# The copies of feed-forward pieces move behind the copy of M on ScalarE, their squares behind c1 on VectorE

## The chip, the cores and the metric

The kernel runs on one core of a Trainium2 chip. The metric is the device time of one execution in microseconds (us), as the median of a few runs. TensorE (PE) multiplies into PSUM; VectorE (DVE) and ScalarE (ACT) read PSUM and SBUF; GpSimd (POOL) works on SBUF only; SyncE (SP) issues DMAs. Each engine carries out its own instructions in the order in which the program issues them, and waits on semaphores for the others.

## What is computed

A recurrence over 768 time steps for 4 batches and 8 heads of size 40, and a feed-forward network behind it:

```
y[t]  = r[t] . state
Sa    = state . a[t]
state = state * w[t] - outer(Sa, b[t]) + outer(v[t], k[t])
x     = y, laid out as 3072 tokens x 320
out   = (relu(x @ w_in) ** 2) @ w_out        # 320 -> 2048 -> 320
```

The inputs and the output are float32. The kernel computes the recurrence in chunks of 128 time steps as matrix products with a triangular system per chunk, and holds most operands as bf16.

## The kernel before

**Tiling.** There are 6 chunks of time. In each chunk the 4 batches times 8 heads are worked off in 8 *steps* of 4 heads, so the main loop (line 490) runs over 48 steps, and two more that drain it. Tile's scheduler is switched off (`manual_schedule`): on every engine the instructions stand in the order in which the Python code issues them.

**A step** issues, in this order:

1. `st_ex_mm` and `st_a_mm`: products for the step before (`ex`, line 341) and for the next one (`ca`, line 242), on PE.
2. the first *filler*: one piece of feed-forward work.
3. `st_y`, `st_ex_ev` (DVE, lines 378, 383 and 349) and `st_z` (PE, line 358) for earlier steps.
4. `st_p`: the products P (PE, lines 258 and 264); `st_m`: ACT copies P to Mc (line 273). This is the "copy of M".
5. `prepare(st, 1)`: in even steps `prep_ga`, which transposes on PE (line 197), copies the result to GT on ACT (line 224) and makes AT from it on DVE (line 225), and `prep_cast` (ACT `lnW`, POOL casts); in odd steps `prep_rv`, which transposes and copies to RV on ACT (line 204, 1.02 us).
6. `st_corr` with Mc (PE, line 280); `st_c1`: DVE makes c1 from P and Mc (line 288); `st_a_ev`: DVE makes CN of the next step (line 250).
7. the second filler.
8. `st_corr` with c1 (PE, line 280); `st_sn`: ACT makes Sn, a part of EVX (line 296), POOL makes x and Cc (lines 299 and 300), ACT sums squares of CN into a junk tile jk (line 302); at the last step of a chunk two longer sums, jm (line 307), follow.
9. the third filler.
10. `prepare(st, 4)`: in even steps `prep_decay`, the product cs (PE, line 179), which ACT turns into GI and G (lines 182 and 184) and POOL into K and B (line 188); in odd steps `prep_kb`, transposes on PE and a copy to KBT on ACT (line 212).
11. `st_t`: transposes tb (PE, lines 316 and 322), the copy SnT (DVE, line 326), the copy UBD (ACT, line 328); `st_kb` (PE, line 368); the gather of X by DMAs on SP and the loads of later batches.

**Feed-forward work.** The output of a chunk goes through the network in two halves of 256 tokens. A half has 12 pieces, which the three fillers of four steps take one by one from step 8 on: eight pieces `ffn_in`, each six matmuls into a PSUM tile `hp` (line 428), a Relu copy by ACT to `hs` (line 433) and a square of `hs` into `Gt` (line 436; pieces 0, 2, 4, 6 on DVE, pieces 1, 3, 5, 7 on POOL); then two output tiles in two pieces each (`ffn_out`, line 454), with the copy `osb` by ACT (line 458) and an output DMA on SP after the second. Below, a step with the pieces 0 to 2 is of kind **A**, with 3 to 5 of kind **B**, with 6, 7 and the first half of an output tile of kind **C**, with the three other output pieces of kind **D**. Steps 8 to 47 are ten times A, B, C, D. The two halves of the last chunk are left: six pieces of the first run in steps 48 and 49, and all others after the loop, where six PSUM tiles are used in turn.

**Squares.** `ffn_in` puts its square in a list, and `flush` issues it when the next filler is called.

**PSUM.** All eight banks are taken. Two of them, the tag `ff`, serve the tiles `hp`, `op_`, `cs` and the transposes of `prep_rv`, `prep_kb` and `prep_ga` (t1, t2, t3). A new tile of that tag takes the bank whose last tile got its last reader first in program order, and its first matmul waits until that reader is done. In the kernel before the sequence is: A: hp, t3, hp, hp, cs; B: hp, t1, hp, hp, t2; C: hp, t3, hp, op_, cs; D: t1, op_, t2.

Of the kernel before, what the change touches and what calls it, by code (L numbers as in the profile page):

```python
# [8 lines left out]
BF16 = mybir.dt.bfloat16  # L9
I32 = mybir.dt.int32  # L10
ALU = mybir.AluOpType
ACTF = mybir.ActivationFunctionType
# [6 lines left out]
def kernel(  # L19
# [21 lines left out]
    nc = tc.nc  # L41

    NB, NHH, T, D = r.shape
    L = 128
# [11 lines left out]
    HB = NB // 2  # L56
# [5 lines left out]
    ffp = ctx.enter_context(tc.tile_pool(name="ffp", bufs=3))  # L62
# [23 lines left out]
    for m in range(AHEAD):  # L86
# [11 lines left out]
        out=UTI[:], in_=ones_f[:], pattern=[[1, 128]],  # L98
# [7 lines left out]
        out=IDb[:], in_=ones_b[:], pattern=[[1, 128]],  # L106
# [3 lines left out]
    for i in range(30):  # L110
# [4 lines left out]
        out=MEX[:], in_=MEX[:], pattern=[[0, 4], [1, L]],  # L115
# [15 lines left out]
    for i in range(4):  # L131
# [5 lines left out]
        for s in range(2):  # L137
            o_ = 64 * s
            nc.vector.tensor_copy(
                out=t_[o_:o_ + D, 0, :, L:LV],  # L140
                in_=IDb[o_:o_ + D, o_:o_ + D].rearrange("p (u d) -> p u d", u=1)
# [126 lines left out]
    def st_m(st):  # L268
        c, q = divmod(st, NQ)
        if q == 0:  # L270
            Mc[c] = chp.tile([128, NQ, 4, D], BF16, name="Mc", tag="Mc")
            Cc[c] = chp.tile([128, NQ, 4, D], BF16, name="Cc", tag="Cc")
        nc.scalar.activation(out=Mc[c][:, q], func=ACTF.Copy,
                             in_=Ps[st][:].rearrange("p i s e -> p (i s) e")[:, :, 0:D])
# [10 lines left out]
    def st_c1(st):  # L285
        c, q = divmod(st, NQ)
        c1 = c1s[st] = qdp.tile([128, 4, D], BF16, name="c1", tag="c1")
        nc.vector.tensor_tensor(out=c1[:],  # L288
                                in0=Ps[st][:].rearrange("p i s e -> p (i s) e")[:, :, 0:D],
                                in1=Mc[c][:, q], op=ALU.subtract)  # L290

    def st_sn(st):
        c, q = divmod(st, NQ)
        P, EVX, c1, CN = Ps.pop(st), EVXs[st % NEV], c1s.pop(st), CNs.pop(st)
        Sn = EVX[:, :, :, L + LV:2 * LV].rearrange("p i s e -> p (i s) e")
        nc.scalar.activation(out=Sn, in_=P[:].rearrange("p i s e -> p (i s) e")[:, :, 0:D],  # L296
                             func=ACTF.Copy, scale=-1.0)
        t_ = qdp.tile([128, 4, D], FP32, name="x1", tag="x1")
        nc.gpsimd.tensor_tensor(out=t_[:], in0=Mc[c][:, q], in1=c1[:], op=ALU.add)  # L299
        nc.gpsimd.tensor_tensor(out=Cc[c][:, q], in0=t_[:], in1=Sn, op=ALU.add)  # L300
        jk = qdp.tile([128, 2, 2, L], BF16, name="jk", tag="jk", bufs=1)
        nc.scalar.activation(out=jk[:], in_=CN[:, :, :, 1, :], func=ACTF.Square,  # L302
                             accum_out=ACC[:, AN + st:AN + st + 1])
        if q == NQ - 1:
            for src, at in ((Mc.pop(c), AM), (Cc.pop(c), AC)):
                jm = qdp.tile([128, NQ, 4, D], BF16, name="jm", tag="jm", bufs=1)
                nc.scalar.activation(out=jm[:], in_=src[:], func=ACTF.Square,  # L307
                                     accum_out=ACC[:, at + c:at + c + 1])
# [23 lines left out]
    def st_ex_mm(st):  # L332
        c, o, j0, p2, EVX = where(st)
        SnT = SnTs.pop(st)
        ex = exs[st] = [ps.tile([128, 2, 2, L], FP32, name=f"ex{s}", tag=f"ex{s}")
                        for s in range(2)]
        for u in range(2):
            for i in range(2):
                for s in range(2):
                    lhsT = SnT[half(s), i, :] if u else o.RV[half(s), 1, j0 + i, 0:L]  # L340
                    nc.tensor.matmul(out=ex[s][:, i, u, :], lhsT=lhsT,  # L341
                                     rhs=o.RV[half(s), 0, j0 + i, 0:L],
                                     start=(i == 0 and u == 0), stop=True, skip_group_check=True)

    def st_ex_ev(st):
        EVX = EVXs[st % NEV]
        ex = exs.pop(st)
        for s in range(2):
            nc.vector.tensor_tensor(  # L349
                out=EVX[:, :, s, 0:2 * LV].rearrange("p i (u x) -> p i u x", u=2)[:, :, :, 0:L],  # L350
                in0=ex[s][:], in1=MEX[:].rearrange("p (i u) x -> p i u x", u=2), op=ALU.mult)
# [59 lines left out]
            engines[h % len(engines)].dma_start(  # L411
                out=X[g][row:row + D], in_=src[:, HB * hf:HB * hf + HB, h // 2, :])

    later = []

    def flush():
        while later:
            later.pop(0)()

    def ffn_in(c, hf, jj):  # L420
        flush()
        if jj == 0:
            Gts[c, hf] = chp.tile([128, NJ, HB, L], BF16, name="Gt", tag="Gt")
        hp = ps.tile([128, 2, HB * L], FP32, name="hp", **where_ff())
        for u in range(2):
            j = 2 * jj + u
            for g in range(3):
                nc.tensor.matmul(out=hp[:, u, :], lhsT=WIN[g][0:rows[g], j * 128:(j + 1) * 128],  # L428
                                 rhs=Xs[c, hf][g][0:rows[g]].rearrange("p a b -> p (a b)"),
                                 start=(g == 0 and u == 0), stop=(g == 2),  # L430
                                 skip_group_check=True)
        hs = ffp.tile([128, 2 * HB * L], BF16, name="hs", tag="hs")
        nc.scalar.activation(out=hs[:], in_=hp[:].rearrange("p u x -> p (u x)"), func=ACTF.Relu)  # L433
        eng = nc.gpsimd if jj % 2 and not tail else nc.vector
        Gt = Gts[c, hf]
        later.append(lambda: eng.tensor_tensor(  # L436
            out=Gt[:, 2 * jj:2 * jj + 2].rearrange("p j a b -> p (j a b)"),
            in0=hs[:], in1=hs[:], op=ALU.mult))

    ops, tail = {}, []  # L440

    def where_ff():
        if not tail:
            return {"tag": "ff", "bufs": 2}
        tail.append(tail.pop(0))
        return {"tag": tail[-1], "bufs": 2} if tail[-1] == "ff" else {"tag": tail[-1]}

    def ffn_out(c, hf, b_, part):
        flush()
        if part == 0:  # L450
            ops[c, hf, b_] = ps.tile([128, DM], FP32, name="op_", **where_ff())
        op_ = ops[c, hf, b_]
        for j in range(part * NJ // 2, (part + 1) * NJ // 2):
            nc.tensor.matmul(out=op_[:], lhsT=Gts[c, hf][:, j, b_, :], rhs=WOUT[:, j, :],  # L454
                             start=(j == 0), stop=(j == NJ - 1))
        if part == 1:
            osb = ffp.tile([128, DM], FP32, name="osb", tag="osb")
            nc.scalar.activation(out=osb[:], in_=op_[:], func=ACTF.Copy)  # L458
            tok = (HB * hf + b_) * T + c * L
            nc.sync.dma_start(out=out[tok:tok + L, :], in_=osb[:])  # L460
# [5 lines left out]
    def filler(st):  # L466
        if fill and fill[0][0] <= st:
            fill.pop(0)[1]()
# [8 lines left out]
    def prepare(st, lot):  # L477
        for f, m in when.pop((st, lot), []):
            f(m)
# [10 lines left out]
    for st in range(NS + 2):  # L490
        if 1 <= st <= NS:
            st_ex_mm(st - 1)
        if st + 1 < NS:
            st_a_mm(st + 1)
        filler(st)
        if st >= 2:
            st_y(st - 2)
        if 1 <= st <= NS:
            st_ex_ev(st - 1)
            st_z(st - 1)  # L500
        if st < NS:
            st_p(st)
            st_m(st)
        prepare(st, 1)
        if st < NS:
            st_corr(st, Mc[st // NQ][:, st % NQ], False)
            st_c1(st)
        if st + 1 < NS:
            st_a_ev(st + 1)
        filler(st)  # L510
        if st < NS:
            st_corr(st, c1s[st], True)
            st_sn(st)
        filler(st)
        prepare(st, 4)
        st_t(st, st - 2)
        if 1 <= st <= NS:
            st_kb(st - 1)
        if st == 1:
            load_win()  # L520
        if st == 4:
            load_wout()
        if st >= 2:
            c, q = divmod(st - 2, NQ)
            hf = q // (NQ // 2)
            if q % (NQ // 2) == NQ // 2 - 1:
                gather(c, hf, [nc.sync] if st < NS + 1 else [nc.sync, nc.gpsimd, nc.sync])
                at = st + (3 if c + 1 < NCH else 2)
                fill += [(at, lambda c=c, hf=hf, j=j: ffn_in(c, hf, j)) for j in range(NJ // 2)]
                fill += [(at, lambda c=c, hf=hf, b_=b_, p_=p_: ffn_out(c, hf, b_, p_))  # L530
                         for b_ in range(HB) for p_ in range(2)]
        prepare(st, 5)
        if st == 3:
            nc.gpsimd.memset(UZs[0][:], 0.0)
    flush()


# [130 lines left out]
```

## Time and profile before

| | |
|---|---|
| time, median of 3 runs | 330.74 us (329.7 to 332.66) |
| the profiled execution | 330.49 us, span 328.8 us |
| busy PE / PE weight loads | 85% / 65% |
| busy DVE / ACT / POOL | 68% / 71% / 57% |
| granted PE clock, whole span | 0.943 |
| granted PE clock, 107 to 155, 155 to 203 and 203 to 251 us | 1.00 |
| eight steps (one chunk) in steady state | 48.0 us |
| PE busy in the 48.0 us from 155 to 203 us | 44.46 us |

The span is the profiled stretch from the first to the last instruction; the execution's own time is 1.7 us longer. Times in the timeline are microseconds from the start of the span. A line of the timeline gives start, length, engine, source line, operation, the tile written and the tiles read, the number of instructions merged, and in brackets how long the engine was idle before and what released it. Ends of matmuls are modelled, and a matmul may start before the one before it is said to end.

The two jm instructions of line 307 mark the end of a chunk: they begin at 155.0 and at 202.9 us, so steps 24 to 31 lie between. Of these, step 28 (kind A) has its first piece at 181.64 us, step 29 (B) at 187.26, step 30 (C) at 192.60, and step 31 (D) begins its first output piece at 198.65.

### The profile page before, as it was taken

What the parts mean: (1) busy time and instruction counts of PE and PEld (TensorE: products, weight loads), DVE (VectorE), ACT (ScalarE), POOL (GpSimd) and SP (SyncE); (2) the same over time, 40 slices, a digit from 0 to 9 for tenths busy, and PEclk for the clock granted to TensorE, in tenths of its full rate; (3) what the DMA queues carried; (4) which work ended last, traced back from release to release, by engine and by line L of the source; (5) the groups of instructions that cost most, each with busy time, mean ns of one, the idle gap of its engine ahead of it and who ended that gap; (6) DMA issues with size and microseconds to landing.
All of it is one profiled execution on the core that took longest, in us unless ns stands there. A gap on an engine that the chain in (4) does not pass through costs nothing.

```text
span 328.8 us, 10009 instructions
## 1 busy us (share of the span) xinstructions
PE 280.4 (85%) x3856; PEld 213.3 (65%) x3856; DVE 222.7 (68%) x545; ACT 232.8 (71%) x569; POOL 188.3 (57%) x342
## 2 busy tenths in 40 slices
PE   4478777799999799999799999899998899888990
PEld 3446555577777577777577777677776677666770
DVE  7226968587787587786686886686876775954430
ACT  3366766886886986887986787886887886538450
POOL 3367757296585485676476676476674673533300
PEclk9555978899999999999999999999999999999997
DMA  8992999985737437635736844735862701000100
GB/s 136 174 165 40 176 165 167 169 126 99 151 71 138 94 69 141 126 69 112 128 55 121 147 82 78 144 62 120 131 106 47 147 18 44 20 23 28 55 22 29
DMA packets 164187, 32.86 MB, mean 100 GB/s; under 512 B 158660, under 2 KB 163780, under 8 KB 164130
## 3 DMA queue, kind: packets, MB, share of 16 engines
q1 hardware_dynamic: 161586, 29.44, 49.7%
q0 software_dynamic: 2544, 2.68, 5.1%
q8 instruction: 32, 0.52, 0.7%
q14 instruction: 25, 0.20, 0.2%
HBM read 28.84 MB, written 3.93 MB: 100 GB/s over the span
## 4 chain that ended last, share of the span: by engine, by line
PE 56%; ACT 18%; issue 7%; DVE 7%; POOL 4%; DMA 3%; SPq 3%; ACTq 0%; DVEq 0%; POOLq 0%
PE hp L428 12%; PE t L197 6%; PE ex L341 4%; PE P L280 4%; PE cs L179 4%; ACT hs L433 3%; ACT jm L307 3%; PE uy L368 3%; ACT RV L204 3%; SPq L81 3%; PE tb L316 3%; PE ca L242 2%; DMA NV<-in_v_dram 2%; DVE c L288 2%; ACT GT L224 2%
## 5 line engine op out<-in xcount | busy, mean ns | idle before, releaser
L428 PE MATMUL hp<-X,WIN 120*128 120x256 bf16 (+1 forms) x576 | 78.9, 275 | 8.1 <-ACT osb L458 6.1
L433 ACT ACTIVATE hs<-hp 128x512 bf16<-128x512 f32 x96 | 57.3, 597 | 26.1 <-PE hp L428 22.7
L349 DVE TENSOR_TENSOR EVX<-ex,MEX 128x512 bf16<-128x512 f32 x96 | 61.8, 686 | 1.7 <-PE ex L341 0.5
L428 PEld LDWEIGHTS <-WIN 120*128 120x128 bf16 (+1 forms) x576 | 50.7, 98 | 18.9 <-issue 9.6
L250 DVE TENSOR_TENSOR CN<-ca,MCN 128x512 bf16<-128x512 f32 x96 | 61.4, 681 | 0.7 <-PE ca L242 0.7
L299 POOL TENSOR_TENSOR x<-Mc,c 128x160 f32<-128x160 bf16 x48 | 23.3, 486 | 66.7 <-DVE c L288 66.6
L436 POOL TENSOR_TENSOR Gt<-hs 128x512 bf16<-128x512 bf16 x43 | 48.4, 1125 | 9.9 <-ACT hs L433 9.6
L454 PEld LDWEIGHTS <-Gt 128*128 128x128 bf16 x384 | 34.3, 97 | 13.4 <-POOL Gt L436 0.8
L280 PEld LDWEIGHTS <-CN 128*128 128x128 bf16 x384 | 23.2, 98 | 27.2 <-issue 23.6
L326 DVE COPY SnT<-tb 128x256 bf16<-128x256 bf16 x48 | 14.0, 291 | 33.3 <-PE tb L322 27.6
L300 POOL TENSOR_TENSOR Cc<-x,EVX 128x160 bf16<-128x160 f32 x48 | 25.3, 527 | 17.1 <-ACT EVX L296 16.8
L436 DVE TENSOR_TENSOR Gt<-hs 128x512 bf16<-128x512 bf16 x53 | 27.4, 519 | 9.4 <-ACT hs L433 9.2
L225 DVE TENSOR_TENSOR AT<-t,GT 128x512 bf16<-128x512 bf16 x24 | 10.2, 425 | 31.4 <-ACT GT L224 31.4
L302 ACT ACTIVATE jk<-CN 128x512 bf16<-128x512 bf16 x48 | 30.1, 627 | 0.0
L212 ACT ACTIVATE KBT<-t 128x1024 bf16<-128x1024 bf16 x24 | 24.6, 1024 | 6.0 <-PE t L197 6.0
L204 ACT ACTIVATE RV<-t 128x1024 bf16<-128x1024 bf16 x24 | 24.6, 1023 | 5.1 <-PE t L197 3.0
L188 POOL TENSOR_TENSOR Kp<-NK,GI 128x320 bf16<-128x320 f32 x24 | 22.4, 933 | 6.6 <-ACT GI L182 5.6
L280 PE MATMUL P<-c,CN 128*128 128x40 bf16 x192 | 12.4, 181 | 13.5 <-DVE c L288 13.5
L288 DVE TENSOR_TENSOR c<-P,Mc 128x160 bf16<-128x160 f32 x48 | 15.3, 319 | 10.4 <-PE P L280 9.6
L378 DVE TENSOR_TENSOR YS<-uy,GT 128x256 bf16<-128x256 f32 x48 | 20.2, 421 | 1.2 <-PE uy L368 0.8
L242 PE MATMUL ca<-AT,KBT 64*128 64x128 bf16 x384 | 20.0, 228 | 1.2 <-DVE AT L225 1.2
L296 ACT ACTIVATE EVX<-P 128x160 bf16<-128x160 f32 x48 | 14.4, 300 | 8.7 <-PE P L280 8.4
(142 smaller groups left out, 636.6 us busy)
## 6 DMA issues: line engine op xcount, KB each, us to landing
NW<-in_w_dram SPq DMA_DIRECT2D x24, 160.0 KB
NK<-in_k_dram SPq DMA_DIRECT2D x24, 160.0 KB
NB<-in_b_dram SPq DMA_DIRECT2D x24, 160.0 KB
NA<-in_a_dram SPq DMA_DIRECT2D x24, 160.0 KB
NV<-in_v_dram SPq DMA_DIRECT2D x24, 160.0 KB
NR<-in_r_dram SPq DMA_DIRECT2D x24, 160.0 KB
out_dram<-osb SPq DMA_DIRECT2D x24, 160.0 KB
X<-YS SPq DMA_DIRECT2D x93, 20.0 KB
```

Of the source, the lines that this page charges most:

```text
L204: nc.scalar.activation(out=o.RV[:, :, :, 0:L], in_=t1[:], func=ACTF.Copy)
L212: nc.scalar.activation(out=o.KBT[:], in_=t2[:], func=ACTF.Copy)
L242: nc.tensor.matmul(out=ca[s][:, i, u, :], lhsT=o.KBT[half(s), u, j0 + i, :], rhs=o.AT[half(s), j0 + i, :], start=(i == 0 and u == 0), stop ...
L250: nc.vector.tensor_tensor(out=CN[:, :, s], in0=ca[s][:], in1=MCN[:], op=ALU.mult)
L280: nc.tensor.matmul(out=P[:, i, s, 0:D], lhsT=CN[:, i, s, 1, :], rhs=X[:, 2 * i + s], start=False, stop=last, skip_group_check=True)
L300: nc.gpsimd.tensor_tensor(out=Cc[c][:, q], in0=t_[:], in1=Sn, op=ALU.add)
L302: nc.scalar.activation(out=jk[:], in_=CN[:, :, :, 1, :], func=ACTF.Square, accum_out=ACC[:, AN + st:AN + st + 1])
L349: nc.vector.tensor_tensor(out=EVX[:, :, s, 0:2 * LV].rearrange("p i (u x) -> p i u x", u=2)[:, :, :, 0:L], in0=ex[s][:], in1=MEX[:].rearra ...
L428: nc.tensor.matmul(out=hp[:, u, :], lhsT=WIN[g][0:rows[g], j * 128:(j + 1) * 128], rhs=Xs[c, hf][g][0:rows[g]].rearrange("p a b -> p (a b) ...
L433: nc.scalar.activation(out=hs[:], in_=hp[:].rearrange("p u x -> p (u x)"), func=ACTF.Relu)
L436: later.append(lambda: eng.tensor_tensor(out=Gt[:, 2 * jj:2 * jj + 2].rearrange("p j a b -> p (j a b)"), in0=hs[:], in1=hs[:], op=ALU.mult))
L454: nc.tensor.matmul(out=op_[:], lhsT=Gts[c, hf][:, j, b_, :], rhs=WOUT[:, j, :], start=(j == 0), stop=(j == NJ - 1))
```

## The change

The Relu copy and the square of a feed-forward piece are no longer issued with its matmuls and at the next filler. Both go through lists of their own. The copies are issued: behind the copy Mc (for the first piece of a step), behind `st_sn`, so behind Sn, jk and jm (for the second piece), and at the next filler, which is the first one of the next step (for the third piece, so behind GI and G or KBT, and behind UBD). The squares are issued behind c1 and ahead of CN (for the third piece of the step before and the first of this one), and right behind the copy of the second piece. Ahead of the second half of an output tile, and after the loop, all squares are issued. `hs` gets four buffers in place of three. What is computed stays the same.

```
+    copies, squares = [], []
+    def flush(*lots):
+        for lot in lots or (copies, squares):
+            while lot:
+                lot.pop(0)()
     def ffn_in(c, hf, jj):
-        flush()
+        flush(copies)
...
-        hs = ffp.tile([128, 2 * HB * L], BF16, name="hs", tag="hs")
-        nc.scalar.activation(out=hs[:], in_=hp[:].rearrange("p u x -> p (u x)"), func=ACTF.Relu)
+        hs = ffp.tile([128, 2 * HB * L], BF16, name="hs", tag="hs", bufs=4)
...
-        later.append(lambda: eng.tensor_tensor(
-            out=Gt[:, 2 * jj:2 * jj + 2].rearrange("p j a b -> p (j a b)"),
-            in0=hs[:], in1=hs[:], op=ALU.mult))
+        def square():
+            eng.tensor_tensor(out=Gt[:, 2 * jj:2 * jj + 2].rearrange("p j a b -> p (j a b)"),
+                              in0=hs[:], in1=hs[:], op=ALU.mult)
+        def copy():
+            nc.scalar.activation(out=hs[:], in_=hp[:].rearrange("p u x -> p (u x)"),
+                                 func=ACTF.Relu)
+            squares.append(square)
+        copies.append(copy)
+        if tail:
+            while len(squares) > 1:
+                squares.pop(0)()
...
     def ffn_out(c, hf, b_, part):
-        flush()
+        flush(copies)
+        if part == 1 or tail:
+            flush(squares)
...
             st_p(st)
             st_m(st)
+        flush(copies)
         prepare(st, 1)
         if st < NS:
             st_corr(st, Mc[st // NQ][:, st % NQ], False)
             st_c1(st)
+        flush(squares)
         if st + 1 < NS:
             st_a_ev(st + 1)
         filler(st)
         if st < NS:
             st_corr(st, c1s[st], True)
             st_sn(st)
+        flush(copies)
+        flush(squares)
         filler(st)
         prepare(st, 4)
```

## The prediction

> **What bounds the kernel now.** I read the page's slices first, then the list of waits, then the timeline of one group of four steps.
>
> ```profile
> PE   4478777799999799999799999899998899888990
> DVE  7226968587787587786686886686876775954430
> ACT  3366766886886986887986787886887886538450
> PEclk9555978899999999999999999999999999999997
> ...
> PE P L280 <- DVE c L288: 13.5, 26, 1.3
> PE P L280 <- ACT Mc L273: 3.9, 17, 0.6
> PE hp L428 <- ACT osb L458: 6.1, 5, 1.2
> ```
>
> From slice 8 on PE is the full engine, and its order is fixed, so what ends a step is PE's last matmul of it. The waits say what is left to gain: PE waited 13.5 us for c1, 7.5 of them in the first 59 us, where no feed-forward work runs, and 3.9 us for Mc. Step 28 (kind A) and the start of step 29 show what a step is made of (PE first, then ACT; start, length):
>
> ```profile
> 182.53 0.26 PE L264 MATMUL P<-EVX,CN 128*128 128x40 bf16 x4
> 182.85 0.39 PE L197 MATMUL t<-IDb,Ap 128*128 128x128 bf16 x4
> 183.41 0.26 PE L280 MATMUL P<-Mc,CN 128*128 128x40 bf16 x4 [0.17 <-ACT Mc L273]
> 184.61 0.26 PE L280 MATMUL P<-c,CN 128*128 128x40 bf16 x4 [0.28 <-DVE c L288]
> 184.72 0.82 PE L428 MATMUL hp<-X,WIN 120*128 120x256 bf16 x6
> 185.38 0.70 PE L179 MATMUL cs<-lnW,UTI 128*128 128x320 f32 x2
> 187.26 0.83 PE L428 MATMUL hp<-X,WIN 120*128 120x256 bf16 x6
> ...
> 183.06 0.30 ACT L273 ACTIVATE Mc<-P 128x160 bf16<-128x160 f32 x1
> 183.27 0.60 ACT L224 ACTIVATE GT<-t 128x512 bf16<-128x512 bf16 x1
> 184.43 0.60 ACT L433 ACTIVATE hs<-hp 128x512 bf16<-128x512 f32 x1 [0.20 <-PE hp L428]
> 184.92 0.30 ACT L296 ACTIVATE EVX<-P 128x160 bf16<-128x160 f32 x1
> 185.11 0.63 ACT L302 ACTIVATE jk<-CN 128x512 bf16<-128x512 bf16 x1
> 185.72 0.60 ACT L433 ACTIVATE hs<-hp 128x512 bf16<-128x512 f32 x1
> ```
>
> PE stands still only 0.17 us for Mc and 0.28 us for c1 here. The copy hs at 184.43 is done before Sn (EVX, 184.92) can start, and cs, at 185.38, finds its PSUM bank free: the bank of `hp` whose copy was that hs. PE never waits for a Relu copy.
>
> **The first piece of a step (kinds A, B, C): copy behind Mc.** In A, Mc now starts 0.29 us after the last four matmuls of P, as with an idle ACT early in the trace (P 35.81, Mc 36.10): 182.82 in place of 183.06. The matmul behind it then waits for the transposes in front of it instead (182.85 + 0.39 = 183.24): 0.17 won. But GT now stands behind the moved copy: Mc occupies ACT for 0.21 (183.06 to 183.27), a copy hs for 0.49 (184.43 to 184.92), so GT starts at 182.82 + 0.70 = 183.52, 0.25 late. AT needs GT, and c1 stands behind AT on DVE; from GT to the c1 matmul it was 184.61 - 183.27 = 1.34. So that matmul comes 0.25 late, and the 0.17 is eaten. The second piece reuses the bank of the first, which is free at 183.03 + 0.60 + 0.05 = 183.68; its 0.82 end before the c1 matmul, so this is hidden there. (0.05 is what lies between the end of a copy and the matmul that waits for it: Mc ends at 183.36, its matmul starts at 183.41.) In B no GT stands between, but the second piece waits: counted from B's first piece (187.26), the copy starts at 1.07 + 0.29 + 0.21 = 1.57 and frees the bank at 2.22; the second piece began at 1.89. 0.33 late.
>
> **The second piece: copy behind Sn and jk.** This is the large term. In A cs must take the bank of the second piece: the third holds the other. Row by row from the c1 matmul: Sn starts 0.31 later (184.61 to 184.92), jk 0.19 after that, the copy 0.61 after jk (185.11 to 185.72, the read of the sum included), lasts 0.60, and PE may go 0.05 later: 1.76. Before, cs came 0.77 after the c1 matmul (A) or, behind the longer output piece, 1.19 (C, 195.58 to 196.77). So A loses 0.99 + 0.25 = 1.24, and C 0.57 + 0.25 = 0.82. On PE everything of the step is queued behind cs: tb, the K and B products, the next step's first piece. On ACT, GI, G and UBD follow; GI's bank is free 0.74 + 0.42 + 0.45 + 0.05 = 1.66 after cs starts, before the next first piece wants one (1.88).
>
> In B it is the transposes t2 that wait. From B's first piece: second piece 2.22, c1 matmul 0.67 later (189.15 to 189.82), 2.89; Sn 3.20, jk 3.39, copy 4.00, t2 at 4.65. Before: 190.81 - 187.26 = 3.55. B loses 1.10. RV, also pushed back, ends at 1.57 + 0.49 + 1.02 = 3.08, some 0.1 after the third piece could start: inside the wait of t2. KBT follows t2 and is out (about 6.4) just when the next first piece can start (4.65 + 0.54 + 1.25 = 6.44); with no slack left, 0.1 more is a risk.
>
> **The third piece: copy behind GI, G or KBT, and UBD.** Its bank is not the next wanted: the next first piece takes that of cs or t2, which is released earlier in the order. The trace shows that banks go by release and don't strictly alternate: in D, t1 follows an output tile and cs, and started at 200.06 while osb, at 199.94 for 0.44, was still reading the older tile. I take 0.
>
> **The squares.** On DVE piece 0 moves ahead of CN, 0.46 us of work in the same stretch, and piece 2 from the start of B behind its c1; CN is wanted a step later, and DVE waited 27.6 us in all for tb, so 0. Piece 4's square now waits for its late copy, with SnT queued behind it, but in B tb is as late. The squares of pieces 1 and 7 on POOL wait too, with K and B behind them, which wait for GI anyway; POOL waited 66.6 us for c1. `hs` with four buffers costs nothing. No DMA is moved; the output copy osb and its DMA on SP keep their place.
>
> **Sum.** A 1.24 + B 1.10 + C 0.82 + D 0 = 3.16 per four steps. Steps 8 to 43 are nine such groups: 28.4. In the first, PE's clock is lower and cs came 1.12 after the c1 matmul: 0.6 less. In steps 44 to 47 cs and t2 are missing; there SnT waits for piece 4's square, about 0.8 (286.49 to some 287.3). Steps 48 and 49 and the rest run ACT in the same order: 0. Together 28.6 on the profiled 330.49, which is 0.25 under the median: **359 us**.
>
> Of what the trace doesn't show, the wait of PE for hs, the bounds are: at least 0.04 behind the end of a copy (GT's end, 183.87, to AT, 183.91) and at most 0.15 (Sn's end, 185.22, to Cc on POOL, 185.37); and the copy may start with the end of jk's main pass, 0.09 sooner. Over three waits in nine groups that is -2.5 to +2.7 us. I take 0.05, the row with the same two engines.
>
> **Two rules of the skill.** PE gets idle gaps of up to 1 us. In this trace a gap of 1.25 us before a piece (158.13) left the granted clock of the stretch from 155 to 203 us at 1.00. The Trainium skill (TensorE: Matmul & The Clock Gate, "A second HAM failure mode: psum-queue depth-cycling") says that frequent micro-idles between matmul groups can make the clock swing to half. As an estimate from that page, half speed on the 44.46 us of PE work per eight steps would add some 200 us in all; by the row it adds 0, and I go by the row. The skill's PSUM — Partial Sum Buffer ("Summary: rules for kernel authors") asks to evacuate promptly; that speaks against this change, gives no size, and no run here shows it yet.
>
> **Rivals.**
> - *Faster*: the chain M, c1, Sn gets ACT and DVE sooner and the freed waits stay freed. Per group: 0.17 + 0.28 in A and in C and about 0.3 in B, 1.2, ten times: 12, so 318. For it: the waits of PE named above. It decides if the late copies are out within 0.77 us of the c1 matmul in A; the rows give 1.76, and GT takes c1's part back. 0.08.
> - *No change*: the order in which ACT gets its work is not what the code suggests, or a slack that I don't see takes up 1 us a step: 330. Against it: PE busy 44.46 of 48.0 us. 0.05.
> - *Part*: in B a bank is free sooner than I have it, and GT's delay is covered: A 0.99 and C 0.57, nine times: 14, so 344. 0.07.
> - *Strict turns*: the next first piece must wait for the third piece's copy. In A that is 0.74 + 0.42 + 0.41 (GI, G, UBD) + 0.26 (UBD 158.88 to hs 159.14) + 0.65 = 2.48 after cs in place of 1.88, in B as much: 1.3 per group, 11.6 more, so 371. The row of D speaks against it. 0.10.
>
> **Numbers.** The forecast, 355 to 363 with its bounds, has 0.70. The range takes in strict turns and most of the way to the partial case: 347 to 373. A measurement of this kernel tells about 1% from no change. Slower by over 1%: 0.87, the forecast, the partial case and strict turns; within: 0.05; faster: 0.08.
>
> **What the next profile should show.** PE's waits for hs of line 433 at cs (A, C) and at t2 (B), 0.6 to 1 us each, 27 in all, some 22 us, and at the second piece of B, 0.3 each; PE waiting for Mc gone; PE's share of the span down from 85% to about 78%; eight steps in 54.3 us in place of 48.0; first pieces not waiting for ACT. I am wrong if PE's wait at cs is short (jk passed by), if the first piece of B and C waits (strict turns), or if the granted clock leaves 1.00.

## The result

The changed kernel takes 361.72 us in the median of 4 runs (359.19 to 363.24), the kernel before 331.05 in the median of 4: a ratio of 1.092, with an interval from 1.083 to 1.100. The forecast was 359 in a range from 347 to 373, slower. The profiled execution of the changed kernel took 360.79 us with a span of 359.0, against 330.49 and 328.8: 30.2 us of span more.

In the page of the changed kernel the slices and the chain show what is no longer full:

```profile
PE   4677777889889789889689889689889698888990
...
ACT  3366758676677776576776676776676776556460
...
PEclk9556858899999999899999999999999999999997
...
PE 53%; ACT 26%; issue 6%; DVE 5%; POOL 3%; DMA 3%; SPq 2%; DVEq 0%; POOLq 0%; ACTq 0%
```

PE was at 9 in most slices from slice 8 on and is now at 8 and 9 with a 6 or 7 in between, and the slices of ACT did not rise for it. The chain that ended last runs over ACT for 26% of the span where it was 18%. The third line is the granted clock, on which more below. Both engines wait for each other more: PE's order holds it at one product, and what that product needs stands late in ACT's order. The list of waits of the changed kernel names it:

```profile
PE P L280 <- DVE c L288: 14.0, 26, 1.2
...
PE cs L179 <- ACT hs L442: 10.9, 18, 0.8
...
PE hp L429 <- ACT hs L442: 6.3, 27, 0.2
...
PE t L197 <- ACT hs L442: 6.0, 9, 0.7
```

The columns are microseconds in total, times, and the longest. The waits for hs did not exist before: PE waits for a Relu copy 18 times at cs (nine groups, A and C), 9 times at the transposes t2 (B), and 27 times at the second piece of a step. The wait for c1 is about as long as before (14.0, before 13.5). In the timeline of one group, steps 28 and 29, the order of the waits can be followed (PE, then ACT):

```profile
199.26 0.83 PE L429 MATMUL hp<-X,WIN 120*128 120x256 bf16 x6
...
201.29 0.82 PE L429 MATMUL hp<-X,WIN 120*128 120x256 bf16 x6 [0.23 <-ACT hs L442]
202.47 0.26 PE L280 MATMUL P<-c,CN 128*128 128x40 bf16 x4 [0.36 <-DVE c L288]
...
204.22 0.81 PE L179 MATMUL cs<-lnW,UTI 128*128 128x320 f32 x2 [0.82 <-ACT hs L442]
...
206.20 0.83 PE L429 MATMUL hp<-X,WIN 120*128 120x256 bf16 x6
...
210.63 0.38 PE L197 MATMUL t<-IDb,Kp 128*128 128x128 bf16 x4 [0.66 <-ACT hs L442]
...
202.77 0.30 ACT L296 ACTIVATE EVX<-P 128x160 bf16<-128x160 f32 x1 [0.69 <-PE P L280]
202.97 0.62 ACT L302 ACTIVATE jk<-CN 128x512 bf16<-128x512 bf16 x1
203.58 0.59 ACT L442 ACTIVATE hs<-hp 128x512 bf16<-128x512 f32 x1
```

From the c1 matmul (202.47) to cs (204.22) there are 1.75 us, through Sn, jk and the copy; before the change there were 0.77. ACT itself was idle for 0.69 us ahead of Sn, with the second piece complete and its copy next but two in the order.

### The profile page after: what moved, and what is told of

It is laid out like the page before. It is cut to its first block, busy times and chain, and to the rows that moved or that the text cites. A ratio compares the mean times of both kernels' runs of the same rounds, so it can differ in the third digit from the quotient of the medians.

```text
span 359.0 us, 9991 instructions
## 1 busy us (share of the span) xinstructions
PE 290.6 (81%) x3856; PEld 218.2 (61%) x3856; DVE 227.9 (63%) x545; ACT 234.1 (65%) x569; POOL 187.8 (52%) x342
## 3 DMA queue, kind: packets, MB, share of 16 engines
HBM read 28.84 MB, written 3.93 MB: 91 GB/s over the span
## 4 chain that ended last, share of the span: by engine, by line
PE 53%; ACT 26%; issue 6%; DVE 5%; POOL 3%; DMA 3%; SPq 2%; DVEq 0%; POOLq 0%; ACTq 0%
PE hp L429 12%; ACT hs L442 8%; ACT jk L302 6%; PE t L197 5%; PE cs L179 5%; PE ex L341 4%; PE P L280 3%; PE uy L368 3%; ACT EVX L296 3%; ACT jm L307 3%; PE ca L242 3%; PE tb L316 3%; ACT Mc L273 2%; SPq L81 2%; DMA NV<-in_v_dram 2%
## 5 line engine op out<-in xcount | busy, mean ns | idle before, releaser
L429 PEld LDWEIGHTS <-WIN 120*128 120x128 bf16 (+1 forms) x576 | 52.6, 97 | 25.2 <-issue 15.6
L299 POOL TENSOR_TENSOR x<-Mc,c 128x160 f32<-128x160 bf16 x48 | 26.1, 544 | 76.7 <-DVE c L288 76.7
L438 POOL TENSOR_TENSOR Gt<-hs 128x512 bf16<-128x512 bf16 x43 | 45.1, 1050 | 33.2 <-ACT hs L442 32.1
L438 DVE TENSOR_TENSOR Gt<-hs 128x512 bf16<-128x512 bf16 x53 | 31.8, 601 | 8.3 <-ACT hs L442 8.2
L273 ACT ACTIVATE Mc<-P 128x160 bf16<-128x160 f32 x48 | 14.5, 302 | 27.5 <-PE P L264 27.5
L179 PE MATMUL cs<-lnW,UTI 128*128 128x320 f32 x48 | 21.9, 542 | 12.3 <-ACT hs L442 10.9
L300 POOL TENSOR_TENSOR Cc<-x,EVX 128x160 bf16<-128x160 f32 x48 | 23.4, 486 | 11.0 <-ACT EVX L296 7.8
L188 POOL TENSOR_TENSOR Kp<-NK,GI 128x320 bf16<-128x320 f32 x24 | 21.0, 874 | 13.5 <-ACT GI L182 12.7
L182 ACT ACTIVATE GI<-cs 128x320 f32<-128x320 f32 x24 | 10.5, 436 | 20.9 <-PE cs L179 20.9
```

The lines of the kernel that those rows point to most:

```text
L179: nc.tensor.matmul(out=cs[:].rearrange("p h e -> p (h e)"), lhsT=UTI[:], rhs=o.lnW[:], start=True, stop=True)
L438: eng.tensor_tensor(out=Gt[:, 2 * jj:2 * jj + 2].rearrange("p j a b -> p (j a b)"), in0=hs[:], in1=hs[:], op=ALU.mult)
```

## The experiments

Each ran beside the kernel before on the same chip, and its ratio is to that. The median of the kernel before lay between 330.2 and 331.4 us in them, so times of different runs can be compared to about 1 us. "Eight steps" is the time from the first jm of one chunk to the first jm of the next: 47.97 us in the kernel before, 54.13 in the changed one.

### One part alone, and one part taken back

`flush(copies)` straight after a filler puts that piece's copy back behind its matmuls. The three places are the fillers of a step; the squares stay where the change put them in all five kernels.

**Only the second copy late**: added after the first and after the third filler.

```
         filler(st)
+        flush(copies)
         if st >= 2:
...
         filler(st)
+        flush(copies)
         prepare(st, 4)
```

> Only the second piece's copy stays behind Sn and jk; the first and third pieces' copies go back behind their matmuls, the squares stay as in the changed kernel. Theory (the bank held by the late second copy): cs and t2 still wait, A loses 0.99, C 0.57, B 0.77, each some 0.1 more because the weights of the waiting product can't be loaded ahead, 0.2 back in B from the moved square: about 2.4 per group, nine groups, so 351 to 354. Rival (GT and c1 behind the first piece's copy are the main cost): nearly all is gone, 331 to 336.

Measured: 352.4 us (351.63 to 354.14), ratio 1.066 (1.062 to 1.071), eight steps 52.85 us. As the theory had it; some two thirds of the loss (21.5 of 30.7 us) are this copy.

**The second copy taken back**: added after the second filler alone.

```
         filler(st)
+        flush(copies)
         if st < NS:
             st_corr(st, c1s[st], True)
```

> The second piece's copy goes back behind its matmuls, ahead of Sn; the first copy stays behind Mc, the third behind UBD, the squares as in the changed kernel. Theory: PE's waits for hs at cs and t2 go; GT's delay stays, 0.25 in A and in C, and the second piece of B waits 0.2: 0.5 to 0.7 per group, so 335 to 338. Rival (first copy is the main cost): 350 or more.

Measured: 338.38 (337.09 to 340.11), ratio 1.025 (1.021 to 1.029). It is at the upper edge of the theory, and 23 us below the changed kernel. Its waits of PE after the first 59 us:

```profile
PE P L280 <- DVE c L288: 6.5, 18, 0.4
PE hp L429 <- ACT hs L442: 6.3, 27, 0.2
```

The waits at cs and t2 are gone, those at the second piece and for c1 are as in the changed kernel. Of the latter, c1 cost 6.0 in 18 waits before the change too; in A and C it is the later start of the c1 matmul, not a longer wait, that the first copy costs.

**Only the first copy late**: `flush(copies)` after the second and the third filler.

> Only the first piece's copy is late (behind Mc); the second and third go back behind their matmuls, the squares stay as in the changed kernel. Theory: the c1 matmul comes 0.24 late in A and in C, the second piece of B waits 0.2 for its bank, so 0.75 per group as in second_back, 337 to 340. Rival (the third copy had a share in second_back): 331 to 334.

Measured: 337.19 (337.03 to 337.8), ratio 1.021 (1.016 to 1.026), eight steps 49.47 us, as with the second copy taken back. So the third copy has no share there.

The size is as expected, the path in B only in part. From first piece to first piece A and C grew by 0.24 and 0.23, as the c1 matmul is later by that much; B grew by 0.29 (5.34 to 5.63). There P starts 0.18 sooner, for piece 2's square has left its place ahead of UZ, and that makes up for most of the wait at the second piece: t2 is only 0.06 later. The rest comes from DVE (a step B of this run, its first piece at 190.63):

```profile
192.80 1.20 DVE L438 TENSOR_TENSOR Gt<-hs 128x512 bf16<-128x512 bf16 x1
...
195.12 0.44 DVE L438 TENSOR_TENSOR Gt<-hs 128x512 bf16<-128x512 bf16 x1
195.49 0.28 DVE L326 COPY SnT<-tb 128x256 bf16<-128x256 bf16 x1
```

The late copy lets POOL's square of piece 3 start (192.68) just ahead of DVE's square of piece 2, which then takes 1.20 us (0.52 in the run with only the squares moved). CN, the next square and SnT follow without a gap, and the product that needs SnT starts 5.19 after the first piece in place of 4.90. In the changed kernel the wait at t2 covers this.

**Only the third copy late**: `flush(copies)` after the first and the second filler.

> Only the third piece's copy is late (at the next step, behind GI, G or KBT, and UBD); the first and second go back behind their matmuls, the squares stay as in the changed kernel. Theory (its bank is not the one the next first piece takes): nothing, as with the squares alone, 329 to 332, and no wait of PE for hs at a first piece. Rival (strict turns): 0.6 in A and in B, 1.2 to 1.3 per group, so 341 to 343.

Measured: 330.64 against 331.38, ratio 0.998 (0.994 to 1.002). PE waits for no Relu copy. The bank of the third piece is not the one that the next first piece takes; strict turns are out. The changed kernel shows it directly: the first piece of step 29 starts at 206.20, while the third copy of step 28 (206.16, 0.61 long) is still reading its bank.

**Only the squares moved**: `flush(copies)` after all three fillers.

> All three copies go back behind their matmuls; only the squares stand where the change put them. Theory: the square of piece 2 no longer stands ahead of YS and UZ in B, PE's wait for UZ (0.28) goes, P starts 0.18 sooner: 1.6 in nine groups, so 329 to 330, a ratio near 0.995. Rival (DVE's order matters as such: CN behind a square holds up the next step): slower than before, 333 or more.

Measured: 330.35 against 330.85, ratio 1.000 (0.998 to 1.002). Neither expectation: nothing that can be told from the kernel before. The trace shows the gain and what eats a part of it. The wait of PE's weight loads for UZ in B (2.7 us in 9 waits before) is gone, P starts 0.18 sooner, and eight steps take 47.67 us in place of 47.97. But in the last eight steps, 45.9 us in place of 45.4, SnT stands behind a square on DVE where no transposes cover it:

```profile
285.37 0.29 PE L341 MATMUL ex<-RV,SnT 64*128 64x128 bf16 x4 [0.59 <-DVE SnT L326]
```

By the marks of the chunks 0.9 us are left of the 1.6, too little for these runs to tell from nothing.

### What the second copy waits for

**Between Sn and jk**: one line in `st_sn`, behind the copy Sn.

```
         nc.scalar.activation(out=Sn, in_=P[:].rearrange("p i s e -> p (i s) e")[:, :, 0:D],
                              func=ACTF.Copy, scale=-1.0)
+        flush(copies)
```

> As the changed kernel, but the second piece's copy is issued between Sn and jk. Theory: the bank is free 0.61 sooner; the wait in A falls from 0.82 to 0.2, in C from 0.40 to 0, in B from 0.66 to 0.05: 1.6 to 1.7 per group, 15 in all, so 346 to 348. Rival (PE waits for Sn's place in the order, not for jk's length): within 3 us of the changed kernel, 359 to 363.

Measured: 342.2 (341.86 to 343.58), ratio 1.036 (1.032 to 1.040), some 4 us better than the theory had it. The waits of PE after the first 59 us show it: 18 waits at cs of 10.9 us became

```profile
PE cs L179 <- ACT hs L443: 1.7, 8, 0.2
```

and those at t2 went. So the sums of squares in jk, which nobody on the path needs, were what held the bank: 0.61 us in front of a copy that PE waits for. Eight steps take 50.49 us, 3.6 less than in the changed kernel, 1.8 per group where 1.6 to 1.7 were expected. Nine groups of that are 16.3 of the 18.3 us by which the span is shorter; 1.5 more are a slow stretch of the clock in the changed kernel's execution (below), which the expectation did not know of.

### What the first copy delays

**c1 ahead of AT**, on the changed kernel: `prep_ga` puts the AT product into a list, which is issued behind `st_c1`.

```
-        nc.vector.tensor_tensor(out=o.AT[:], in0=t3[:, 1], in1=o.GT[:, :, 0:L], op=ALU.mult)
+        ats.append(lambda: nc.vector.tensor_tensor(
+            out=o.AT[:], in0=t3[:, 1], in1=o.GT[:, :, 0:L], op=ALU.mult))
...
             st_c1(st)
+        while ats:
+            ats.pop(0)()
```

> As the changed kernel, but on VectorE c1 is issued ahead of AT. Theory (the first copy pushes GT back, GT holds AT, AT holds c1): PE's 0.36 us waits for c1 in A and C go, the c1 matmul starts 0.5 sooner, and with it Sn, jk and the late copy: 0.4 to 0.5 in 19 steps, so 352 to 355. Rival (c1 is late by its own inputs): 359 to 363.

Measured: 348.72 (348.17 to 351.53), ratio 1.055 (1.049 to 1.062): 13 us less than the changed kernel, where 7 to 10 were expected. One step of kind A of this run:

```profile
192.45 0.82 PE L434 MATMUL hp<-X,WIN 120*128 120x256 bf16 x6 [0.23 <-ACT hs L447]
193.11 0.26 PE L285 MATMUL P<-c,CN 128*128 128x40 bf16 x4
...
194.86 0.81 PE L179 MATMUL cs<-lnW,UTI 128*128 128x320 f32 x2 [0.63 <-ACT hs L447]
```

The wait for c1 is gone, the c1 matmul follows the second piece after 0.66 us, where it took 1.18. Eight steps take 52.06 us, 2.07 less, which is 0.52 in each A and C as expected. Three chunks of that, 1.6 in the first chunk with pieces and 1.3 in the last eight steps make 9.1 us from the order, in the upper part of the expectation. Of the rest, 1.5 us in one execution and 3 in another are slow stretches of the clock in the changed kernel (below), which are absent here, where the clock stayed at 1.00 from 72 to 300 us. The start differs too, and from one execution to the next: jm of the first chunk starts at 57.12 us here, and at 59.81 and 57.20 in two executions of the changed kernel.

### A faster kernel

The same reading, ACT's sums ahead of a copy that frees a bank, fits a wait that was there before the change: PE's first piece of a chunk waits 1.25 us for osb, which stands behind two jm.

**The sums jm later**, on the kernel before: `st_sn` keeps the two sums of a chunk in a list, and one is issued ahead of the first filler of a step of kind D, where ACT was idle for 1.22 us ahead of osb; the last chunk keeps them where they were. The edit where a sum is issued:

```
+        if sums and st < NS and st % 4 == 3:
+            st_sum()
         filler(st)
         if st >= 2:
             st_y(st - 2)
```

> The kernel before with one edit: the two long sums jm of a chunk are not issued behind jk of its last step but one at a time ahead of the first output copy in later steps of kind D, where ScalarE stands idle for 1.2 us. Theory (what PE waits for is a copy that frees a bank, and sums that nobody waits for stand ahead of it): the 1.25 us wait for osb at four chunk starts goes and A falls from 7.30 to 5.62 there, 1.68 times 4, so 323 to 326. Rival (the first piece of a chunk waits for something else too): 329 to 331.

Measured: 323.3 (322.78 to 325.31), ratio 0.976 (0.971 to 0.980), as the theory had it. Eight steps take 46.28 us in place of 47.97, 1.69 less, which is 6.8 in four chunks; the medians differ by 8.1. Of PE's five waits for osb the one behind the last chunk is left:

```profile
PE hp L436 <- ACT osb L466: 1.1, 1, 1.1
```

**All of it**: the copies behind their matmuls, the squares as in the changed kernel, c1 ahead of AT, jm later.

> All three copies behind their matmuls, the squares as in the changed kernel, c1 ahead of AT, and the sums jm in later steps as in jm_later. Theory: jm 6.7, c1 sooner in 20 steps by 0.3 (then the copy of the second piece is what cs waits for), so 315 to 321. Rival (PE already bound by its own work): 324 or more.

Measured: 318.27 (317.75 to 318.71), ratio 0.961 (0.957 to 0.966), the fastest kernel here. After the first 59 us PE waits for these:

```profile
PE P L285 <- ACT Mc L278: 4.9, 21, 0.6
PE hp L442 <- ACT osb L484: 1.1, 1, 1.1
...
PE P L285 <- DVE c L293: 0.4, 2, 0.2
```

The 6.0 us for c1 fell to 0.4, the 6.1 for osb to 1.1. The 4.9 for Mc, 0.17 in nearly every A and C, are what the change was after; they are what is left once the larger waits are gone. The run with the first copy alone shows that this copy costs more behind Mc than it frees, there with AT ahead of c1; it was not run with c1 ahead of AT and the second copy in its old place. Nor was c1 ahead of AT run alone on the kernel before: the 5.0 us from the run with jm later to this one are its share and that of the squares together.

### The clock

The changed kernel's first profile had one step in which every matmul was slow. So it was run once more.

> The changed kernel once more, for the clock: its profile had one stretch of 3.6 us at half the PE clock behind a wait at cs, 1.5 us of time. If the gaps make the clock swing, it shows again at such a wait, and eight steps take more than 54.1 us somewhere; if it was chance, all full groups of eight steps take 54.1.

Measured: 361.96 us, one execution. Four of its cs, two of them slow (PE, start, length, wait ahead):

```profile
93.39 1.43 PE L179 MATMUL cs<-lnW,UTI 128*128 128x320 f32 x2 [0.82 <-ACT hs L442]
...
108.02 0.81 PE L179 MATMUL cs<-lnW,UTI 128*128 128x320 f32 x2 [0.40 <-ACT hs L442]
...
231.07 0.81 PE L179 MATMUL cs<-lnW,UTI 128*128 128x320 f32 x2 [0.82 <-ACT hs L442]
...
257.30 1.44 PE L179 MATMUL cs<-lnW,UTI 128*128 128x320 f32 x2 [0.82 <-ACT hs L442]
```

In the stretch from 257.3 to 261.0 the granted clock was 0.55, in the 7 us ahead of it 1.00; the eight steps around it took 55.59 us where the two chunks ahead of them took 54.1. The first profile of the changed kernel has the same, 0.53 from 148.6 to 152.2, behind a wait of 0.82 at cs, and also 55.59 us for its eight steps. So it came more than once: one such stretch in the first execution, two in the second, 1.5 us each. It does not come with every long wait: the wait of the same length at 231.07 left the clock alone, and in the run with only the second copy late, which waits 0.82 there too, the granted clock was 1.00 from 72 to 300 us. From 74 to 300 us no other kernel here, ten in all with the one before, has such a stretch. That the waits cause it is therefore likely but not shown; when it strikes stays open.

## Why the prediction was right, and where it was off

**Order of the waits.** The forecast named the wait at cs and t2 as the large term. The runs with this copy alone (1.066) and without it (1.025) bear it out.

**The sizes.** Measured from first piece to first piece, A grew by 1.32 (5.62 to 6.94; forecast 1.24), B by 0.88 (5.34 to 6.22; forecast 1.10), C by 0.89 (6.04 to 6.94; forecast 0.82): 3.09 per group for 3.16. That the sum comes this close is in part luck: B was priced 0.22 too high, A and C together 0.15 too low. Eight steps take 54.13 us for the forecast 54.3.

- *A and C, the first copy*: the c1 matmul comes 3.21 after the first piece, before 2.97: 0.24 for the forecast 0.25. The chain from it to cs was 1.75 in A and 1.74 in C for 1.76.
- *A and C, what was missed*: cs itself. It took 0.70 with its bank free and takes 0.81 behind a wait, for its weights are loaded only when the wait ends: the load starts with the product (both at 204.22), where it started 0.11 ahead of it before (185.27 and 185.38). The run with the copy between Sn and jk gives the same 0.81 behind a wait of 0.21.
- *B, what was over-priced*: I had the second piece start 0.33 late; it was 2.03 after the first in place of 1.89, so 0.14. The step that failed is the one on the squares, taken at 0: piece 2's square no longer stands ahead of UZ on DVE, P starts 0.18 sooner in B, and the late copy with it. The squares alone show these 0.18 by themselves.
- *The third copy*: 0, as forecast. *Strict turns* is out by the run of that copy alone.
- *The last group*: from its first piece to the end of its fourth step 20.84 us in place of 20.02, so 0.8 as forecast, with a wait of 1.2 for SnT, as named.
- *The clock*: forecast at 0 by the row of one gap of 1.25 us; it was one stretch of 1.5 us in one profile and two in the other. So one of the three signs of being wrong came about, a granted clock that leaves 1.00, at 1.5 to 3 of some 30 us. The Trainium skill (TensorE: Matmul & The Clock Gate, "A second HAM failure mode: psum-queue depth-cycling") says that frequent micro-idles between matmul groups made the clock swing in a kernel there. The two profiles show a swing, at most twice in nine groups, so this speaks for the rule's sign and against the size that I had worked out from it. I had weighed one row against a rule about many gaps; that row could not decide it.

**Sum of the profiled span.** The first chunk with pieces grew by 5.52 (forecast 5.7), the next three by 7.63, 6.16 and 6.17 (6.3 each; the first of them holds the 1.5 of the clock), the last by 3.93 (4.0): 29.41 for 28.6, and 27.9 without the clock. The stage before them was 1.40 longer and the end 0.61 shorter; both differ from one execution to the next (in the second execution of the changed kernel the first is 1.21 shorter and the second 0.25 longer than before).

**The signs named for the profile.** PE's waits for hs at cs, t2 and B's second piece were to be some 22 us and 0.3 a piece. They were 27, as forecast, but 16.9 us in all (0.82 each in A, 0.40 in C, 0.66 in B), and 6.3 at the second pieces of A, B and C, 0.23 each. PE's waits for Mc are gone but for three in the last group (1.2 us), and first pieces wait for no Relu copy. PE's share is 81%, not 78%: its busy time grew from 280.4 to 290.6 us, which the forecast had taken as fixed. In eight steps at full clock it grew from 44.43 to 46.05 (154.95 to 202.92 us before, 223.63 to 277.76 after). 0.41 of that are the four cs. The rest is overlap that is gone: without a wait a product starts before the one ahead of it is said to end (cs at 185.38, the piece ahead of it until 185.54), behind a wait it doesn't, and eight steps have 18 waits in place of 9.

*The rivals.* Faster was to be decided by whether the late copy is out within 0.77 us of the c1 matmul: it took 1.75. Its premise, that waits for c1 hold PE, is true: issuing c1 ahead of AT took 13 us from the changed kernel, 9 of them by the order. The change leaves those waits as they were. *Part* had the bank in B free sooner, which is true by 0.2 us, but B still grew by 0.88, and GT's delay is not covered: the c1 matmul is 0.24 late in A and C.

## What to carry to other kernels

A copy out of PSUM does two things: it hands a value on, and it frees a bank. Before moving one back in its engine's order, count tiles until its bank is wanted again: here the second piece's was wanted at once, the third's not, and the two moves cost 21.5 us and nothing. Then look at what now stands behind the copy: the first piece's cost 7 us, though each wait for its bank was short (0.23), by what it pushed back. What belongs behind everything is work whose result and buffers nobody waits for, such as the sums jk and jm: placing jm was worth 8 us in the kernel before, and putting the second copy ahead of jk 16 of the 31 that the change costs. Both stand in the list of waits, as a wait for the copy behind them.

## What the runs showed of the hardware that was not expected

- PE's granted clock fell to about a half for some 3.6 us once in one profile of the changed kernel and twice in the other, each time at a cs behind a wait of 0.82 us. In six other runs (only the first and only the second copy late, the second taken back, the copy ahead of jk, c1 ahead of AT, and the fastest kernel) it was 1.00 from 72 to 300 us.
- The float32 product cs takes 0.81 us in place of 0.70 when PE has waited for its bank, as its weights then start to load with it and otherwise 0.11 ahead of it.
- The same square on DVE takes 0.41 or 1.20 us. The long one starts 0.12 us after POOL has begun to square another piece (DVE, then POOL, of the changed kernel):

```profile
208.38 1.20 DVE L438 TENSOR_TENSOR Gt<-hs 128x512 bf16<-128x512 bf16 x1
...
210.70 0.41 DVE L438 TENSOR_TENSOR Gt<-hs 128x512 bf16<-128x512 bf16 x1
...
208.26 1.04 POOL L438 TENSOR_TENSOR Gt<-hs 128x512 bf16<-128x512 bf16 x1 [0.90 <-ACT hs L442]
```

  The Trainium skill (Advanced Engine Details and Errata, "Mode Summary") has VectorE's second SBUF port shared with GpSimd, so that GpSimd instructions and VectorE instructions in a two-port mode block each other. The rows agree with a block: the long square ends at 209.58, 0.28 after POOL's (209.30). In which mode the squares run, no run here shows. The change had put the two squares side by side; in its B PE shows no wait for it. In the two runs with the first copy late and the second not, it holds up SnT, as told above.
